# Cross attention with state and a routed MoE on one core: six x tiles, four transposed ones that lend their first to the state, and a redrawn order of work

## The chip, the cores and the metric

The kernel runs on one core of one Trainium2 chip. A core has five engines that run side by side and meet through semaphores: TensorE (PE in the profile; its weight loads are listed apart as PEld), VectorE (DVE), ScalarE (ACT), GpSimd (POOL) and SyncE (SP), which here only issues DMAs. Each engine executes its own instructions in the order in which the program has them, so an instruction that waits holds up everything behind it on its engine. The metric is the device time of one execution in microseconds (us). The kernel before takes 752.19 us as the median of three runs (751.41 to 753.65).

## The reference

Two stages follow each other. In the first, every one of 8 batches and 8 heads has 512 tokens `x` and 32 state rows, 64 wide; the tokens read from the state and the state reads from the tokens. In the second, the 4352 rows that result, 512 wide, pass through 8 experts, weighted by a Sinkhorn-normalised gate over all rows.

```python
scores = scale * x @ state^T;   a  = softmax(scores);   xread = a  @ state
scores2 = scale * state @ x^T;  a2 = softmax(scores2);  sread = a2 @ x
x = concat([xread, sread]) as (B*(512+32), H*64)         # 4352 x 512
P = exp(logits - logits.max());  logits = x @ w_gate     # over all rows
for _ in range(8):
    P /= P.sum(1) + 1e-9;  P /= P.sum(0) + 1e-9;  P *= N / E
out = sum over e of  P[:, e] * (relu(x @ w1[e]) @ w2[e])
```

The result does not need `xread` itself: `xread @ w1` is `a @ (state @ w1)`. The kernel multiplies state and w1 once per expert and batch (V) and uses the transposed softmax `aT` as the other factor; the gate goes the same way with G, which is state times the gate's weights.

## The kernel before, in words

**Two halves.** The first half, some 135 us, is the attention of all batches together with the whole of expert 0 and the beginning of expert 1. Its order on every engine is written out by hand in a table, `PLAN`: each entry is the number of an operation and a letter for its engine (P TensorE, V VectorE, A ScalarE, G GpSimd, S the SP queue, H bookkeeping without an instruction). `issue` (L105) walks through the table. The operations are built by calls of `op` with the engines that may take them and a price for each; the prices serve whoever draws the table, and no instruction depends on them. The second half, experts 1 to 7, is an ordinary loop at the end of the program: for each expert and block of rows, `layer2` forms seven half-size products instead of eight (A, E and Bseed in the profile), while `layer1` and `project` feed the next block.

**Attention.** For a batch `b`, two loads on the GpSimd queue (L468) bring x as fp16 into a tile `x_nat`. There are four such tiles. x is transposed to `xT` (three tiles): by TensorE for the first two batches (L578, with copies out of PSUM), by DMA transposes on the SP queue for the others (L591). A batch is worked on in two parts of four heads. For each part TensorE forms scores (psB, L605). VectorE then transposes them in blocks (L628), takes the maximum (L631), subtracts it (`subA`, L648); ScalarE takes the exponential (L656), VectorE the sum and its reciprocal, and VectorE or GpSimd multiplies (`a`, L670). VectorE turns the result into `aT` (L674). On the other side VectorE takes a maximum over the scores in PSUM (L640), ScalarE the exponential E with its sum (L652), VectorE the reciprocal (L659), and VectorE or GpSimd scales E (`normB`, L662). A DMA transpose on the SP queue turns E into ETs (L742), and TensorE reads the state's new rows with it (su, L758), which `keepS` (L764) copies into `xsT`. The two parts of the first batch take a direct way: TensorE forms the scores a second time in the other layout (psA, L684) and transposes `a` itself (L709).

**State and weights.** The state is loaded into `st_st`, cast into `st_in` (both tiles of their own in a pool `spl`, L435), and transposed by TensorE into `stT` (L492). Expert 0's weights come in four loads on the GpSimd queue (`weights_ops`, L535): w1 in two, w2 in two.

**Expert 0.** V is formed by TensorE (v_ps, L870) and copied out by ScalarE or VectorE; hidden products (hps, L897) are copied out through a relu into `hT` (L425, L427); the second layer (yps, L935) is copied into `acc`.

**Gate and Sinkhorn.** After all `aT` and su, the last of the gate products (L788, the one on `xsT`) gives the last logits. Then VectorE takes the global maximum (lmx, L814) and runs eight rounds: `rownorm` (five instructions on VectorE as one operation), a product with ones on TensorE (csb, L846), `colnorm` (three instructions as one operation). `sums_w` (L959) forms on VectorE the eight sums of expert 1's second weight that the seven products need.

**PSUM.** In the first half six banks are shared in turn by all products other than psB: a product takes the bank whose last reader was issued longest ago. In the second half there are fixed banks A, E, B0 and B1 and four for hidden products. `seed` (L351) opens B0 and B1 with a product of the identity; ScalarE then copies A over B0 (L363).

**The end.** `layer2_last` (L299) finishes the state's rows: two groups of 128 rows, the second in two halves of the columns, with VectorE adding into `acc` (L314) and eight DMAs of 64 KB on the SP and ScalarE queues, four for each group of rows (L317).

Of the kernel before, what the change touches and what calls it, by code (L numbers as in the profile page):

```python
# [17 lines left out]
46V 62P 50H 51G 61A 71V 63P 60A 52G 64V 11G 72V 73A 80P 65V 12G 435P 401P 66A 81V 13H 79P 14G 82V 436A 88V  # L18
437A 404P 83A 67V 402A 137H 403A 89V 96H 97P 100P 84V 406A 68V 90A 98A 15G 85V 69P 86P 53G 405A 99V 87V 70A
103P 101A 102A 91V 409P 16H 92G 413P 104V 407P 410A 411P 105V 111A 438P 120P 414V 408A 419P 421P 106V 415P  # L20
112V 138S 121V 74V 439A 412A 422V 113V 417P 107A 54G 440A 75G 122V 432P 429P 123V 370V 420A 469P 128A 418A
416A 17G 108V 140P 124A 125V 423P 426P 471A 433P 114A 148V 93S 129V 430P 149V 172H 424P 76S 434A 115V 470A
109G 130V 139S 110V 126G 141V 131A 427P 18G 127V 142V 428V 431A 445P 143V 132V 94P 150A 95V 77P 425A 156P 116G
447P 151V 133V 78V 449P 446A 443P 441P 144A 455P 164V 152G 448A 117S 19H 450V 157V 444A 165V 173S 442A 451P
456A 166A 134S 20G 452A 453P 463P 158V 472P 207H 145V 175P 159V 183V 184V 457P 31G 146G 454A 176V 473A 160A
464P 185A 174S 460P 458P 461P 465A 147V 161V 21G 153S 177V 191P 47P 162G 474A 118P 167V 459A 154P 462A 178V
163V 135P 49A 168G 199V 22H 48V 179A 466P 136A 352P 475P 200V 192V 201A 193V 119V 467P 476A 194V 23G 195A 485P
202V 208S 210P 180V 169S 155A 218V 356P 353A 481P 357V 468A 487P 219V 24G 489P 181G 186V 211V 242H 486A 482A
477P 490V 488A 483P 479P 220A 170P 478A 503P 187G 480A 484V 171A 203G 196V 537P 209S 25H 212V 226P 197G 504A
505A 506P 213V 500P 182V 198V 26G 234V 221V 507A 222V 204S 188S 491P 27G 538A 227V 539A 501P 497P 502A 508A  # L30
492P 235V 243S 228V 244S 214A 229V 511P 215V 236A 523P 230A 498P 494P 216G 245P 495P 515P 512V 499A 277H 231V
524A 493A 517P 246V 253V 223S 496A 247V 521P 516A 237V 254V 519P 509P 522V 518A 248V 513P 232G 189P 520A 255A
205P 510V 224P 514V 540P 28H 278S 261P 249A 190V 269V 29G 225A 270V 262V 531P 534P 206V 238G 250V 532P 256V
358P 271A 535P 217V 541A 533A 233V 542A 312H 279S 263V 272V 536A 354P 280P 528P 543P 529P 525P 288V 289V 251G
555P 264V 281V 265A 282V 239S 257V 526P 359A 266V 544A 530V 556A 545P 355A 547P 549P 273G 553P 527A 546V 571P
313S 290A 548A 283V 605P 550A 554V 296P 267G 606V 304V 572A 305V 240P 573A 557P 284A 607A 558A 551P 297V 552A
568P 360P 258S 241V 285V 30G 291V 306A 559P 562P 574P 298V 252V 315P 299V 286V 569P 576A 268V 323V 563P 575A
274S 300A 560P 570A 292G 316V 361A 561A 581P 564A 307V 565P 362P 324V 317V 301V 325A 302G 566P 363V 582A 326V
579P 587P 583P 287V 314S 588V 591P 567A 580A 639P 608P 584A 592A 347H 303V 331P 577P 348G 641V 640A 610A 609A
339V 293S 589P 585P 275P 332V 259P 578A 327G 586A 260A 590A 294P 340V 308G 333V 341A 593P 309S 318V 319A 334V  # L40
295V 364P 594P 276V 328S 625P 619P 342V 595A 335A 365A 599P 320V 602P 343V 336V 600P 337V 603P 626A 321G 322V
329P 310P 350G 344S 601A 349G 311A 620V 345P 338V 346V 604V 366P 596P 330A 368P 369V 351G 597P 367A 371V 611P
372P 598A 695H 615P 617P 373V 612V 374P 375V 613P 614V 616A 623P 618A 621P 696H 711H 376A 705P 377V 642P 624A
622A 706A 707A 630P 643V 697V 708P 644A 378P 379V 631P 710A 627P 698V 380V 647P 632A 709A 636P 628P 381P 633P
699V 648V 637P 382V 634P 657P 629A 638A 383V 700V 653P 658A 655P 384P 651P 635A 701V 654A 725P 385V 723P 386V
702V 656A 726A 716P 652A 724A 717A 645P 659P 649P 714P 646A 650A 660A 387P 721P 715A 712P 727P 687P 722A 388V
728A 688A 667P 713A 664P 389V 390P 703V 665P 668P 391V 673P 674A 392V 661P 670P 669A 729V 393P 671P 394V 666A
662P 672A 677P 395V 718P 663A 678A 679P 675P 683P 719A 681P 720V 680A 676A 685P 396P 684A 682A 397V 686A 692P
704V 689P 693P 690P 730P 398V 694A 399P 733P 731V 691A 732A 735A 734A 400V
# [68 lines left out]
def kernel(  # L118
# [63 lines left out]
    outs = out.rearrange("(b s) d -> b s d", s=SB)[:, S:, :]  # L182
# [32 lines left out]
    axp = actx.enter_context(tc.tile_pool(name="attn_x", bufs=4))  # L215
    axt = actx.enter_context(tc.tile_pool(name="attn_xt", bufs=3))
# [46 lines left out]
    def layer1(e, bi):  # L263
# [35 lines left out]
    def layer2_last():  # L299
# [4 lines left out]
        nb = 128 // Ns  # L304
        for row in range(tn // 128):
# [10 lines left out]
            for i in range(nb):  # L316
                (nc.scalar if i % 2 else nc.sync).dma_start(  # L317
                    out=outs[row * nb + i], in_=acc[ds(i * Ns, Ns), k, :])

    def layer2(e, bi, n):  # L320
# [30 lines left out]
        def seed(i):  # L351
            bb = bank([128, 2, DH], FP32, "Bseed", "B%d" % i)
            nc.tensor.matmul(bb.rearrange("p c d -> p (c d)"), identh, aT[:, 0, 0], start=True, stop=True)
            seeds.append(bb)

        if not n:
            for k, eng in enumerate(("DVE", "ACT", "DVE", "POOL")):
                weigh(k, eng)
        product(A, h(0, 0), w2h[:, :NJ, :DH], True)
        if not n:  # L360
            seed(0)
        Bb = seeds[n % 2]
        nc.scalar.copy(out=Bb[:, :nk], in_=A[:, :nk])  # L363
        yield
        product(Eb, s(0), T[:, 0], True)
        if not n:
            seed(1)
# [67 lines left out]
    st_in = spl.tile([128, B, NQ, 2, D], FP16, name="st_in")  # L435
    st_st = spl.tile([128, B, NQ, D], FP32, name="st_st")
    loads = []
    for g in range(2):
        def load(g=g):
            bs = ds(g * B // 2, B // 2)  # L440
            (nc.scalar if g else nc.sync).dma_start(
                out=st_st[:, bs], in_=state[bs].rearrange("b (q h) n d -> (h n) b q d", q=NQ))

        loads.append(dma((0, 0), 1.0, load, lands=2.7))
        ops[-1].since, ops[-1].hard = 0.5, 1
# [14 lines left out]
    xn = [slot(axp, 4, [128, H, NSC * D], FP16, "x_nat") for _ in range(B)]  # L460
# [18 lines left out]
    for g in range(2):  # L479
        for s_ in range(2):  # L480
# [4 lines left out]
            bd.append(op((0, 0, g), {"DVE": (0.50, 0.64)} if s_ else {"ACT": (0.50, 0.65)}, place, loads[g:g + 1] + warmed))  # L485
    stT_ready = []
    for g in range(4):
# [10 lines left out]
        t = op((0, 1, g), {"PE": (0.35, 0.55)}, turn, bd[g // 2 * 2:g // 2 * 2 + 2] + [makeh], [ps])  # L498
# [68 lines left out]
    for b in range(B):  # L567
        xT = slot(axt, 3, [128, H * NSC // 2, 128], FP16, "xT")
# [29 lines left out]
        for q in range(NQ):  # L598
# [62 lines left out]
            def normB(eng, E2=E2, rrec=rrec):  # L661
                engines[eng].tensor_scalar(out=E2.tile, in0=E2.tile, scalar1=rrec.tile, scalar2=None,  # L662
                                           op0=ALU.mult)
# [59 lines left out]
            n2 = op(r(3), {"DVE": (0.10, 0.25)}, biasB, [m2], [nsB], [nmB])  # L723
# [5 lines left out]
            f2 = op(r(6), {"DVE": (0.16, 0.26)}, recB, [e2], [rrec], [rowsum])  # L729
            f2 = op(r(6), {"DVE": (0.35, 0.48), "POOL": (1.56, 1.70)} if POOLB else {"DVE": (0.35, 0.48)}, normB, [f2], [], [E2, rrec])  # L730
# [33 lines left out]
            def keepS(eng, b=b, q=q, su=su):  # L764
                copy(eng, xsT[:, ds(2 * q, 2), ds(b * Ns, Ns)], su.tile)
# [38 lines left out]
    def sk(on, emit, after, **how):  # L804
        return op(rank, on, lambda _: emit(), after, **how)
# [6 lines left out]
    op((30.0,), {"DVE": (0.2, 0.3)}, lambda _: nc.vector.memset(ones128, 1.0))  # L812
# [8 lines left out]
    c = sk({"PE": (0.18, 0.45)}, lambda: nc.tensor.matmul(gb.tile, ones128[0:1, :], sm_["gm"]), [c], takes=[gb])  # L821
# [4 lines left out]
    for it in range(8):  # L826
        def rownorm():
            rsum = tile_of("rsum", [128, NTB])
            nc.vector.reduce_sum(out=rsum, in_=Pmat, axis=AX_X)
            nc.vector.tensor_scalar(out=rsum, in0=rsum, scalar1=EPS, scalar2=None, op0=ALU.add)  # L830
# [279 lines left out]
```

## Time and profile before

| what | value |
|---|---|
| median of three runs | 752.19 us (751.41 to 753.65) |
| the profiled execution: its time | 752.75 us |
| the profiled execution: its span | 751.0 us |
| TensorE busy | 736.0 us (98%) |
| VectorE busy | 617.0 us (82%) |
| ScalarE busy | 517.7 us (69%) |
| GpSimd busy | 70.8 us (9%) |
| first transpose of x on TensorE | 6.86 us |
| first hidden product of expert 0 (L897) | 18.86 us |
| last gate product (on xsT) begins | 99.47 us |
| first product on A of expert 1 | 135.14 us |
| last addition into acc begins | 747.02 us |

The span is the time between the first and the last instruction of the profiled execution; the time around it is 1.75 us. A row of the list of groups names the line, the engine, the operation, and output and inputs by the program's names with their shapes and the number of instructions; then come their busy time, the mean of one in ns, and the idle time of the engine just ahead of them with what ended it. In the timeline the two first columns are the start and the length in us of neighbouring instructions that were merged. PEclk is the share of its full speed at which TensorE's clock was granted; where no record has been made yet it is shown as full.

### The profile page before, as it was taken

How to read it: one execution, taken by the hardware profiler on the slowest of the kernel's cores; microseconds unless marked ns; L12 is line 12 of the kernel's file. 1: busy time of each engine (PE TensorE's matmuls, PEld its weight loads, DVE VectorE, ACT ScalarE, POOL GpSimd, SP SyncE). 2: the span in 40 equal slices, each digit the busy share in tenths (PEclk: the TensorE clock that was granted, in tenths of full speed). 3: DMA queues.
4: the chain of work that ended last, by engine and by line, in shares of the span. 5: the costliest groups of instructions: out<-in, count | busy, mean ns of one | idle time of the engine just before them, and what ended most of it. 6: DMA issues, size and time to landing. Idle time of an engine off the chain costs nothing.

```text
span 751.0 us, 16151 instructions
## 1 busy us (share of the span) xinstructions
PE 736.0 (98%) x6517; PEld 502.2 (67%) x6517; DVE 617.0 (82%) x1529; ACT 517.7 (69%) x1014; POOL 70.8 (9%) x81
## 2 busy tenths in 40 slices
PE   5999999999999999999999999999999999999997
PEld 3444445666777777776776767776777767767776
DVE  5899989877888789788888788887897888887885
ACT  6876856799876766667666766667666676667662
POOL 4674410200010000100000000100001000000000
PEclk9899999999999999999999999999999999999999
DMA  9997560600033000700007000330007000002234
GB/s 179 140 134 131 82 99 1 109 6 1 1 61 53 2 1 2 113 1 2 1 2 112 2 1 1 58 57 1 1 2 112 2 1 2 1 31 94 103 113 141
DMA packets 51323, 36.71 MB, mean 49 GB/s; under 512 B 25392, under 2 KB 43824, under 8 KB 51248
## 3 DMA queue, kind: packets, MB, share of 16 engines
q0 software_dynamic: 22272, 20.97, 18.5%
q1 hardware_dynamic: 27744, 14.18, 7.6%
q8 instruction: 51, 0.84, 0.5%
q10 hardware_dynamic: 1232, 0.52, 0.3%
q14 instruction: 24, 0.20, 0.1%
HBM read 42.48 MB, written 8.91 MB: 68 GB/s over the span
## 4 chain that ended last, share of the span: by engine, by line
PE 92%; DVE 3%; DMA 1%; ACT 1%; POOL 1%; issue 0%; SPq 0%; POOLq 0%; DVEq 0%; ACTq 0%
PE hps L255 28%; PE Bseed L334 20%; PE A L334 14%; PE E L334 14%; PE yps L935 6%; PE hps L897 4%; PE v_ps L235 4%; DMA xT<-x_nat 1%; DMA x_nat<-in_x_dram 1%; PE y L312 0%; PE v_ps L870 0%; POOL a L670 0%; ACT Hm L275 0%; DVE acc L348 0%; POOL E L662 0%; PE su_ps L758 0%
## 5 line engine op out<-in xcount | busy, mean ns | idle before, releaser
L275 ACT ACTIVATE Hm<-hps 128x512 f16<-128x512 f32 (+1 forms) x496 | 265.8, 577 | 130.5 <-PE hps L255 128.1
L255 PE MATMUL hps<-aT,V 128*128 128x512 f16 x880 | 230.6, 379 | 0.0
L334 PEld LDWEIGHTS <-Hm 128*128 128x128 f16 x1888 | 181.6, 98 | 71.3 <-issue 15.9
L348 DVE SCALAR_TENSOR_TENSOR acc<-Bseed,Pmat,acc 128x256 f32<-128x256 f32 x354 | 155.0, 477 | 9.8 <-PE Bseed L334 6.9
L334 PEld LDWEIGHTS <-sm 128*128 128x128 f16 x1416 | 138.3, 98 | 34.5 <-issue 0.3
L334 PE MATMUL A<-w2h,Hm 128*128 128x256 f16 x944 | 123.7, 273 | 0.0
L334 PE MATMUL Bseed<-T,Hm 128*128 128x256 f16 x944 | 123.3, 273 | 0.0
L255 PEld LDWEIGHTS <-V 128*128 128x128 f16 x880 | 86.1, 98 | 50.8
L348 DVE SCALAR_TENSOR_TENSOR acc<-E,Pmat,acc 128x256 f32<-128x256 f32 x236 | 103.2, 476 | 13.8 <-PE E L334 13.5
L281 DVE TENSOR_TENSOR sm<-Hm 128x512 f16<-128x512 f16 (+1 forms) x122 | 50.1, 411 | 60.4 <-ACT Hm L275 60.2
L243 ACT CAST V<-v_ps 128x512 f16<-128x512 f32 x144 | 74.2, 612 | 0.0
L348 DVE SCALAR_TENSOR_TENSOR acc<-A,Pmat,acc 128x256 f32<-128x256 f32 x118 | 51.9, 479 | 17.9 <-PE A L334 17.6
L935 PE MATMUL yps<-w2h,hT 128*128 128x512 f16 x272 | 64.1, 379 | 0.1
L334 PE MATMUL E<-w2h,sm 128*128 128x256 f16 x472 | 61.7, 273 | 0.0
L334 PE MATMUL E<-T,sm 128*128 128x256 f16 x472 | 61.6, 273 | 0.0
L334 PE MATMUL Bseed<-T,sm 128*128 128x256 f16 x472 | 61.5, 272 | 0.0
L363 ACT COPY Bseed<-A 128x512 f32<-128x512 f32 (+1 forms) x62 | 34.1, 550 | 37.9 <-PE A L334 35.3
L282 DVE TENSOR_TENSOR Hm<-Hm 128x512 f16<-128x512 f16 (+1 forms) x122 | 50.3, 412 | 4.2
L284 DVE TENSOR_TENSOR sm<-Hm,sm 128x512 f16<-128x512 f16 (+1 forms) x122 | 50.2, 412 | 4.2
L283 DVE TENSOR_TENSOR sm<-sm,Hm 128x512 f16<-128x512 f16 (+1 forms) x122 | 49.4, 405 | 0.0
L194 POOL DMA_DIRECT2D w1h<-in_moe_w_dram x12 | 8.5, 714 | 396.9 <-PE hps L255 396.5
L935 PEld LDWEIGHTS <-hT 128*128 128x128 f16 x272 | 25.4, 99 | 28.9 <-issue 1.8
(127 smaller groups left out, 617.7 us busy)
## 6 DMA issues: line engine op xcount, KB each, us to landing
w1h<-in_moe_w_dram POOLq DMA_DIRECT2D x16, 512.0 KB, 7.0
w2h<-in_moe_w_dram POOLq DMA_DIRECT2D x16, 512.0 KB, 8.4
out_dram<-acc SPq DMA_DIRECT2D x32, 256.0 KB, 2.5
x_nat<-in_x_dram POOLq DMA_DIRECT2D x16, 256.0 KB, 5.6
st_st<-in_state_dram ACTq DMA_DIRECT2D x1, 256.0 KB, 4.9
st_st<-in_state_dram SPq DMA_DIRECT2D x1, 256.0 KB, 4.2
ETs<-E SPq DMA_TRANSPOSE x16, 4.3
out_dram<-acc SPq DMA_DIRECT2D x4, 64.0 KB, 1.8
```

Source lines behind the costliest of these rows:

```text
L235: nc.tensor.matmul(ps[q][ds(j * Ns, Ns), :], stT[ds(r, 64), bi, q, ds((j ^ q) * Ns, Ns)], w1h[ds(r, 64), 2 * q + j // 2, cols], tile_posit ...
L243: nc.scalar.copy(out=dst, in_=src)
L255: nc.tensor.matmul(out, lhs, rhs, start=(k == 0), stop=(k == len(terms) - 1))
L275: nc.scalar.activation(out=Hm[:, i, j, :tn], in_=hps[:, :tn], func=AF.Relu)
L281: nc.vector.tensor_add(s1, a21, a22)
L282: nc.vector.tensor_sub(a21, a11, a21)
L283: nc.vector.tensor_sub(s2, s1, a11)
L284: nc.vector.tensor_sub(s4, a12, s2)
L334: nc.tensor.matmul(dst[:, c], lhs(j, c), rhs[:, j], start=first and c == 0 and j == 0, stop=(j == NJ - 1), skip_group_check=True)
L348: nc.vector.scalar_tensor_tensor(out=dst, in0=src[:, c], scalar=p[:, k], in1=dst, op0=ALU.mult, op1=ALU.add)
L363: nc.scalar.copy(out=Bb[:, :nk], in_=A[:, :nk])
L935: nc.tensor.matmul(yps.tile, hT[fb].tile[:, ds(tk * 128, 128)], w2h[:, fb, :], start=(fb == 0), stop=(fb == NFB - 1))
```

## The change

The changed kernel differs in these points:

- `attn_x` has six tiles and `attn_xt` four. `st_st` takes the first turn in the ring of x tiles, `st_in` the first in the ring of xT tiles; the pool `spl` holds neither any more.
- The table is another one. In it expert 0's two loads of w2 stand behind each other on the GpSimd queue, with nothing but the making of the 32-bit identity between them; before, an E product of GpSimd stood between them.
- `issue` puts products of the identity with itself ahead of five operations (`IDLE`): 50 ahead of the first turning of x, 3 ahead of each of the two psA products, 14 ahead of a v_ps product and 5 ahead of the first aT transposes. They are transposes where the PSUM tile is fp16 (the 50 and the 5) and plain products where it is fp32 (the 3, 3 and 14). Their results are overwritten.
- GpSimd may do `subA`, and the table gives it all 14 of them; `normB` on GpSimd is a product of two tensors with the reciprocal broadcast, no longer a product with a scalar per row; six of the eight T sums go to GpSimd.
- Sinkhorn's rounds are single operations, one for each instruction, so that the table can put other work between them.
- `seed` is gone. The first hidden product of the second half is formed in B0 (`lent`), and the copy of A to B0 follows its relu.
- The state's rows are kept in `xsT` in another order, so that a group of 128 rows leaves in one DMA: one for the first group, two, one for each half of the columns, for the second.

```diff
-def issue(ops):
+def issue(ops, idle):
     for step in PLAN:
...
+        idle(op.takes[0].tile if op.takes else None, IDLE.get(int(step[:-1]), 0))
         op.emit(ENGINES[step[-1]])
...
+IDLE = {56: 50, 63: 3, 80: 3, 452: 14, 69: 5}
...
-    axp = actx.enter_context(tc.tile_pool(name="attn_x", bufs=4))
-    axt = actx.enter_context(tc.tile_pool(name="attn_xt", bufs=3))
+    axp = actx.enter_context(tc.tile_pool(name="attn_x", bufs=6))
+    axt = actx.enter_context(tc.tile_pool(name="attn_xt", bufs=4))
...
-    def layer1(e, bi):
+    def layer1(e, bi, lent=None):
...
-                hps = bank([128, S], FP32, "hps", "h")
+                if lent is None:
+                    hps = bank([128, S], FP32, "hps", "h")
+                else:
+                    hps, lent = lent, None
...
-            for i in range(nb):
-                (nc.scalar if i % 2 else nc.sync).dma_start(
-                    out=outs[row * nb + i], in_=acc[ds(i * Ns, Ns), k, :])
+                (nc.scalar if c + 1 < parts else nc.sync).dma_start(
+                    out=outs[row, :, :, cols], in_=acc[:, k, cols])
...
-        def seed(i):
-            bb = bank([128, 2, DH], FP32, "Bseed", "B%d" % i)
-            nc.tensor.matmul(bb.rearrange("p c d -> p (c d)"), identh, aT[:, 0, 0], start=True, stop=True)
-            seeds.append(bb)
...
-    st_in = spl.tile([128, B, NQ, 2, D], FP16, name="st_in")
-    st_st = spl.tile([128, B, NQ, D], FP32, name="st_st")
+    early = [Slot(rings.setdefault("xT", Ring(4)),
+                  lambda: axt.tile([128, B, NQ, 2, D], FP16, name="st_in", tag="xT")),
+             Slot(rings.setdefault("x_nat", Ring(6)),
+                  lambda: axp.tile([128, B, NQ, D], FP32, name="st_st", tag="x_nat"))]
...
             def normB(eng, E2=E2, rrec=rrec):
-                engines[eng].tensor_scalar(out=E2.tile, in0=E2.tile, scalar1=rrec.tile, scalar2=None,
-                                           op0=ALU.mult)
+                if eng == "POOL":
+                    nc.gpsimd.tensor_mul(E2.tile, E2.tile, rrec.tile.broadcast_to((128, S)))
+                else:
+                    nc.vector.tensor_scalar(out=E2.tile, in0=E2.tile, scalar1=rrec.tile, scalar2=None, op0=ALU.mult)
...
-                s1 = op(r(4), {"DVE": (0.60, 0.80)}, subA, [m1], [], [eA, mxA])
+                s1 = op(r(4), {"DVE": (0.60, 0.80), "POOL": (1.05, 1.20)}, subA, [m1], [], [eA, mxA])
...
-        c = sk({"DVE": (2.10, 2.25)}, rownorm, [c])
+        for emit, us, tail in ((row_sums, 0.43, 0.03), (row_eps, 0.20, 0.03), (row_rec, 0.37, 0.03),
+                               (row_mul, 0.45, 0.03), (col_part, 0.62, 0.15)):
+            c = sk({"DVE": (us, us + tail)}, emit, [c])
...
-        nc.vector.tensor_sub(T[:, i, jj], p[:, jj], q[:, jj])
+        engines[eng].tensor_sub(T[:, i, jj], p[:, jj], q[:, jj])
...
+    def idle(t, n):
+        if not n:
+            return
+        t = t.rearrange({2: "p a -> p a", 3: "p a b -> p (a b)", 4: "p a b c -> p (a b c)"}[len(t.shape)])[:, :128]
+        for _ in range(n):
+            if t.dtype == FP16:
+                nc.tensor.transpose(t, identh, identh)
+            else:
+                nc.tensor.matmul(t, identh, identh, start=True, stop=True, skip_group_check=True)
```

More of the change, by code (lines that the diff above doesn't have):

```diff
@@ L459 @@
     makeh.since, makeh.hard = 0.7, 1
-    xn = [slot(axp, 4, [128, H, NSC * D], FP16, "x_nat") for _ in range(B)]
+    xn = [slot(axp, 6, [128, H, NSC * D], FP16, "x_nat") for _ in range(B)]
     x_ready = []
@@ L811 @@
     part("ones")
[L812 removed]
+    ones = op((30.0,), {"DVE": (0.1, 0.25)}, lambda _: nc.vector.memset(ones128, 1.0))
     part("K")
@@ L970 @@
     tdone = op((due_1, 1), {"HOST": (0.0, 0.0)}, make_t, [room] + w2_ready(1))
[L971 to L974 removed]
+    for g in range(2):
+        tg = []
+        for i in range(4):
+            tg.append(op((due_1, 1), {"DVE": (0.42, 0.52), "POOL": (1.06, 1.20)}, lambda eng, i=i, g=g: sums_w(eng, i, g),
+                         [tdone] + tg[i - 1:i] * (i == 1) + tg[1:2] * (i == 3)))
+            tg[-1].goal = -0.9
     for bi in range(2):
@@ L1055 @@
             next(v, None)
+        if not i:
+            seeds += [bank([128, 2, DH], FP32, "Bseed", "B%d" % k) for k in range(2)]
         l2 = layer2(e, bi, i)
-        l1 = layer1(*work[i + 1]) if i + 1 < len(work) and work[i + 1] not in hid else iter(())
+        l1 = iter(())
+        if i + 1 < len(work) and work[i + 1] not in hid:
+            l1 = layer1(*work[i + 1], None if i else seeds[0].rearrange("p c d -> p (c d)"))
+        if not i:
+            next(l2)
+            next(l1)
         for k in range(7):
```

152 lines of the change are left out of this document (80 added, 72 removed).

## The prediction

> **What bounds the kernel now.** I read the page's table by engine first, then its slices, then the busy time by stretches of 10 us, the same for TensorE by single microseconds, the list of waits, the timelines of the first 60 us and of the end, and last the groups by line.
>
> ```profile
> PE 736.0 (98%) x6517; PEld 502.2 (67%) x6517; DVE 617.0 (82%) x1529; ACT 517.7 (69%) x1014; POOL 70.8 (9%) x81
> ...
> PEclk9899999999999999999999999999999999999999
> ```
> TensorE (PE) is busy in all but 15 us. Those 15 us, and the slices where the granted clock is under full, are what an edit ahead of the second expert can win; from 135 us on both programs issue nearly the same TensorE work.
>
> ```profile
> 10.00:20.00 10.00, 7.86 (x96) 4.29 (x94) 9.05 (x22) 8.50 (x19) 0.83 (x1) 0.80 1.35 201
> 20.00:30.00 10.00, 10.00 (x68) 3.73 (x67) 8.29 (x21) 7.53 (x16) 6.10 (x7) 0.86 1.10 154
> 30.00:40.00 10.00, 10.00 (x97) 4.65 (x96) 9.67 (x23) 9.15 (x20) 7.03 (x8) 1.00 0.91 112
> 50.00:60.00 10.00, 8.99 (x83) 3.83 (x80) 9.77 (x20) 7.37 (x17) 5.40 (x6) 1.00 1.03 134
> ```
> (Stretch, length, busy PE, PEld, DVE, ACT, POOL, clock, DMA share, GB/s.) Behind 20 us VectorE (DVE) is nearly as full as TensorE: 93% busy from 30 to 100 us. Two engines share the bound of the attention stage, and relief for one alone buys little.
>
> ```profile
> 15.00:16.00 1.00, 0.25 (x5) 0.97 1.45 195
> 16.00:17.00 1.00, 1.00 (x8) 0.50 1.44 194
> 22.00:23.00 1.00, 1.00 (x19) 0.62 1.16 210
> 14.63 0.62 PE L578 MATMUL xT_ps<-identh,x_nat 128*128 128x128 f16 x8
> 16.00 1.03 PE L578 MATMUL xT_ps<-identh,x_nat 128*128 128x128 f16 x8 [0.76 <-DMA x_nat<-in_x_dram]
> 18.86 3.57 PE L897 MATMUL hps<-aT,V 128*128 128x512 f16 x8
> ```
> After thin work at 13 to 16 us the clock falls to 0.50 at about 15.95 and is back at 22.76. Eight transposes cost 0.62 us warm, 1.03 cold; the first hidden products take 3.5 us up to the next group (22.36), where eight of them at 86.59 take 1.73.
>
> ```profile
> PE xT_ps L578 <- DMA x_nat<-in_x_dram: 7.6, 2, 6.9
> PE psB L605 <- DMA xT<-x_nat: 1.3, 2, 0.9
> PE v_ps L870 <- ACT V L419: 0.5, 1, 0.5
> 41.96 1.17 DVE L648 TENSOR_TENSOR eA<-eA,mxA 128x512 f32<-128x512 f32 x1
> L648 DVE TENSOR_TENSOR eA<-eA,mxA 128x512 f32<-128x512 f32 x14 | 10.4, 746 | 0.1
> L662 POOL TENSOR_SCALAR E<-E,rrec 128x512 f16<-128x512 f16 x12 | 19.2, 1600 | 19.5 <-DVE rrec L659 15.3 <-ACT hT L425 4.0
> L670 POOL TENSOR_TENSOR a<-eA,rA 128x512 f16<-128x512 f32 x12 | 12.8, 1066 | 21.6 <-DVE rA L667 12.9 <-DVE logits L421 4.2 <-ACT logits L419 2.4
> 746.06 2.30 SPq L317 DMA_DIRECT2D out_dram<-acc  x4
> 747.02 0.48 DVE L314 SCALAR_TENSOR_TENSOR acc<-y,Pmat,acc 128x256 f32<-128x256 f32 x1 [0.39 <-PE y L312]
> ```
> TensorE's waits after 6.86 us, when the first x lands, sum to under 5 us.
>
> **The change part by part.** The profiled execution took 752.75 us (span 751.0 and 1.75 around it), 0.56 above the median of 752.19. The sum is made against 752.75.
>
> *Fillers and the first 23 us.* 50 transposes of the identity are put ahead of the first turning of x. The identity is made by 1.29 us; at the cold 107 ns each (16 state transposes from 7.68 to 9.39) they end by 6.7, before x lands at 6.86: no cost. Later 6+14 plain products and 5 transposes go into gaps. If the clock then holds, the eight hidden products cost 1.73 instead of 3.50 and the eight v_ps beside them 0.23 instead of 0.40: 1.9 won. In the new order the 64 small G products (0.72 us at 42.5 us) and 16 more v_ps (about 0.6) run before the first hidden product: 1.3 of later work done in slack. But ScalarE now has eight V evictions before the copy of aT that hidden products wait for, not six (2 x 0.53 more), and one xT copy less (0.63), and the second turning of block 1 waits for an eviction to free its bank: they start 0.4 to 0.9 later than 18.86, I take 0.7. The six fillers at psA hold the first max up by about 0.2. Sum -1.9 -1.3 +0.7 +0.2 = **-2.3**. Ends: -0.8 if the spell stays (three cold microseconds, half lost), -3.3 if the clock is up from the first x on.
>
> The evidence on what wakes the clock is thin. TensorE is transposing for most of 16.00 to 18.45 and the clock stays at 0.50 until 22.76, after hidden products have run for a while; the warm stretch before it followed psB, psA and v_ps products. That speaks for plain products. The Trainium skill (TensorE: Matmul & The Clock Gate, Part 4: PE-mode transpose) says that transposes do not count as activity for the gate; the trace leans that way. By that rule the 50 would wake nothing, and the term would lie between -0.8 and -2.3.
>
> *Work moved between engines ahead of the last gate product (99.47 us).* Counted from both orders, up to the global max of the logits: VectorE loses 14 subtractions (10.4 us), two hidden evictions (1.4) and an xsT copy (0.2); it gains four `a` products (4 x 0.67), two E products (2 x 0.33) and three xT copies (3 x 0.42). That is 7.4 us by mean rows. The rows overlap at their ends (they sum to 95.3 for 85.1 busy), so 6.7. ScalarE loses four acc copies, two hidden evictions, one V copy and three xT copies, near 6. TensorE issues 28 fewer yps, 6 fewer hps and 16 fewer v_ps there: 28 x 0.216 + 6 x 0.216 + 0.6 = 7.9 us, which now stands behind the gate. So the gate must come 7.9 us earlier only to break even. VectorE was 85.1 us busy up to 100, 83.5 of it in the 91.8 us behind 8.35 (91%); at that density the 76.8 us left end near 92. TensorE's work behind its first hidden product, counted at warm spacing (0.216 for 512 columns), filled 96.6% of the time to the gate with the cold loss taken out; at that density the gate comes at 88. That is 7.4 or 11 us earlier. With both nearly full I take the middle: against TensorE's pace **+1.2** of idle. Ends: 0 and, with VectorE alone as the pace, +3.5; with a starving chain more (below).
>
> POOL gets those 14 subtractions at about 1.05 us (L670) and 10 E products whose form changes: 1.60 each before; a tensor product of the same size took 1.07, so between 1.05 and 1.6, and I take 1.07. With 20 DMA issues of 0.8 us that is near 50 us of POOL's first 90. Behind a subtraction that waits for VectorE's max, on the one POOL queue, stand the x loads and the E products that the SP queue's transposes wait for.
>
> *Six x tiles and four xT tiles.* Loads and DMA transposes may run one block further ahead. In before, SP issues the second transpose of block 2 at 26.83 us behind two ETs transposes; now it stands behind one. The waits of psB for xT (1.3) and for E (0.3) may go: **-1.0**, ends 0 and -1.6. The second half of w2 is issued at about 8 us, not 20.70; no listed wait names it, so 0; should it crowd out x of block 1, the cover is gone and TensorE's wait at 16.00 (0.76) grows by at most its own transfer, 3 us.
>
> *Sinkhorn in single steps; T sums on POOL (6 of 8).* Behind the gate TensorE now has 41 us of work, VectorE 36 by rows and ScalarE 26, where it was 33, 34 and 25 in 35.7 us. The eight rounds (30 us) get room: **-0.5**, ends 0 and -1.3 (the excess of that stretch).
>
> *Handing over.* Two seed products go (0.22 each), one hidden group is drawn forward into a seed bank, and the copy into that bank now waits for its relu (0.6): **-0.3**, ends +0.3 and -0.5. *End.* Behind the last acc product one DMA is issued on SP instead of two in turn (0.58 each), but of 128 KB instead of 64 (landings 2.5 at 256 KB, 1.8 at 64): **-0.3**, ends +0.2 and -0.6.
>
> Sum: -2.3 +1.2 -1.0 -0.5 -0.3 -0.3 = -3.2: 752.75 - 3.2 = **749.5 us**, 2.7 under the median.
>
> **The rivals.**
> - *POOL starves VectorE (slower).* A subtraction is 0.4 us longer on POOL and may stand behind a 0.8 us issue or a 1.07 us product. For it: POOL in order, half full. Against: two pairs are in flight. If VectorE stands still 0.4 us for each of 14 pairs, the idle term is 5.6 instead of 1.2: 753.9; with a collision of 0.49 us (the subtraction at 41.96 took 1.17 while POOL ran L670) for four of the eight `a` products left on VectorE, 755.9. I name it **755**. It decides when the last gate product comes less than about 5 us earlier than 99.47. The Trainium skill (SBUF — State Buffer, on the shared port pair) states the collision as a lock: a VectorE operation with two SBUF inputs and a POOL operation that reads SBUF exclude each other. Two of the 14 subtractions, at 1.17 us, agree.
> - *VectorE sets the pace, as dense as before.* Idle +3.5 instead of +1.2: **751.8**. For it: 93% busy; against: 6.7 us less of it.
> - *The fillers do not hold the clock.* The spell stays and the first term is -0.8: **751.0**. For it: 2.5 us of mostly transposes at 16 us left the clock at 0.50, and 55 of the 75 fillers are transposes; against: 14 plain products fall just where the thin work was.
> - *All named waits go.* -3.3, 0, -1.6, -1.3, -0.5, -0.6: -7.3, **745.5**. Against: TensorE was nearly full behind 23 us, and POOL's chain is longer.
>
> **How the numbers follow.** My forecast 0.40 (own range 747.3 to 751), VectorE's pace 0.16, POOL 0.18, the cold clock 0.12, all waits gone 0.14. Two runs differ by up to 2.2 us, so a measurement tells about 0.3% (2.3 us) from no change: under 749.9 is faster, over 754.4 slower. Faster: the 0.14 and most of the forecast, 0.52; slower: POOL's 0.18; within: 0.30. The range 745.7 to 754.8 leaves out 2 in 10.
>
> **What would show it.** Right: no 0.50 rows between 16 and 23 us; last gate product near 90 us; first product on A near 132 to 133; VectorE's subtraction group gone and POOL near 60 us busier work before 100; one DMA behind the last acc product. Wrong: `eA` waits on POOL in VectorE's or ScalarE's list, a gate product after 94 us, clock 0.50 after 16 us, or psB still waiting for xT.

## The result and the profile after

The changed kernel takes 754.27 us (median of 22 runs, 751.98 to 759.49); the kernel before, run beside it on the same chip, takes 752.62 (22 runs, 751.41 to 754.26). The ratio is 1.0031, with a 95% interval of 1.0020 to 1.0042: slower by 0.3%. The forecast was 749.5 us, faster than before.

The profiled execution of the changed kernel took 751.98 us (span 750.2), which is the fastest of its 22 runs and by no means a typical one. Three more profiles of the same kernel, from the runs below, have spans of 753.6, 752.4 and 753.0. All four are used in what follows.

First the page of the changed kernel, its table by engine and the row of the granted clock:

```profile
PE 737.9 (98%) x6590; PEld 506.0 (67%) x6590; DVE 612.6 (82%) x1523; ACT 514.8 (69%) x1006; POOL 78.8 (11%) x95
...
PEclk9999999999999999999999999999999999999999
```

VectorE lost 4.4 us in all and GpSimd gained 8. No slice of the clock is under nine tenths any more. In the stretches of 10 us (columns as in the prediction) the change of place is seen:

```profile
10.00:20.00 10.00, 6.97 (x171) 4.46 (x171) 9.38 (x23) 8.84 (x20) 1.74 (x2) 1.00 1.35 201
20.00:30.00 10.00, 7.20 (x60) 2.98 (x58) 6.68 (x17) 5.88 (x13) 6.72 (x8) 0.96 1.43 146
30.00:40.00 10.00, 10.00 (x99) 4.43 (x98) 8.21 (x21) 7.53 (x18) 5.62 (x6) 0.87 1.43 170
```

The clock is full from 10 to 20 us, where it was 0.80. But from 20 to 30 us TensorE is busy for 7.20 us only, where it had been busy throughout, and behind that the clock falls. The DMA engines' share is 1.43 in the two stretches from 20 to 40, where it was 1.10 and 0.91 (it adds up the times of all packets over 16 engines, so it can pass 1). TensorE's timeline names the place:

```profile
28.25 0.30 PE L612 MATMUL psB<-xT,stT 64*32 64x256 f16 x8 [2.80 <-DMA xT<-x_nat]
```

And its list of waits behind 7 us (us in total, times, longest):

```profile
PE psB L612 <- DMA xT<-x_nat: 3.4, 2, 2.8
PE v_ps L893 <- DMA w1h<-in_moe_w_dram: 1.9, 2, 1.6
PE xT_ps L585 <- DMA x_nat<-in_x_dram: 0.7, 1, 0.7
```

TensorE comes to the first scores of block 2 at 25.45 us, and waits 2.8 us for the DMA transpose of that block's x. The kernel before came there at 26.77 and did not wait; its row names no wait:

```profile
26.77 0.29 PE L605 MATMUL psB<-xT,stT 64*32 64x256 f16 x8
```

The four profiles agree on this place (psB at 28.25, 28.41, 28.5 and 28.3) and differ behind it: the last gate product comes at 91.79, 95.22, 94.02 and 94.58 us. From there to the first product on A it is 42.89 us in each of them. So what spreads the times of this kernel lies ahead of the gate.

Two of the groups that moved, up to 100 us:

```profile
L655 POOL TENSOR_TENSOR eA<-eA,mxA 128x512 f32<-128x512 f32 x14 | 14.6, 1046 | 20.7 <-DVE mxA L638 16.6 <-DVE nsB L651 3.7 <-DVE rrec L666 0.2
L670 POOL TENSOR_TENSOR E<-E,rrec 128x512 f16<-128x512 f16 x10 | 10.4, 1043 | 10.9 <-DVE rrec L666 10.1 <-issue 0.5
```

And from the end of the timeline, the last DMAs of the SP queue:

```profile
745.34 2.05 SPq L323 DMA_DIRECT2D out_dram<-acc  x2
```

The subtractions on GpSimd take 1046 ns and the E products, now a product of two tensors, 1043 instead of 1600, both as forecast. GpSimd waits for VectorE, and not the other way round. At the end two DMAs are issued on SP where there were four, and one on ScalarE's queue where there were four.

### The profile page after: what moved, and what is told of

It reads as the page before. It is cut to its first block, busy times and chain, and to the rows that moved or that the text cites. A ratio compares the mean times of both kernels' runs of the same rounds, so it can differ in the third digit from the quotient of the medians.

```text
span 750.2 us, 16283 instructions
## 1 busy us (share of the span) xinstructions
PE 737.9 (98%) x6590; PEld 506.0 (67%) x6590; DVE 612.6 (82%) x1523; ACT 514.8 (69%) x1006; POOL 78.8 (11%) x95
## 3 DMA queue, kind: packets, MB, share of 16 engines
q0 software_dynamic: 22272, 20.97, 19.1%
## 4 chain that ended last, share of the span: by engine, by line
PE 92%; DMA 4%; DVE 1%; POOL 1%; ACT 1%; issue 0%; POOLq 0%
PE hps L260 28%; PE Bseed L340 20%; PE A L340 14%; PE E L340 14%; PE yps L958 7%; PE hps L920 4%; PE v_ps L240 4%; DMA x_nat<-in_x_dram 3%; DMA xT<-x_nat 1%; PE su_ps L767 1%; PE y L319 0%; PE v_ps L893 0%; DVE acc L354 0%; ACT Hm L283 0%; POOL x_nat L475 0%; PE gate_ps L797 0%
## 5 line engine op out<-in xcount | busy, mean ns | idle before, releaser
L354 DVE SCALAR_TENSOR_TENSOR acc<-E,Pmat,acc 128x256 f32<-128x256 f32 x236 | 103.2, 477 | 14.5 <-PE E L340 14.3
L958 PE MATMUL yps<-w2h,hT 128*128 128x512 f16 x272 | 65.9, 386 | 0.1
```

The costliest lines, as they stand in the source:

```text
L354: nc.vector.scalar_tensor_tensor(out=dst, in0=src[:, c], scalar=p[:, k], in1=dst, op0=ALU.mult, op1=ALU.add)
L958: nc.tensor.matmul(yps.tile, hT[fb].tile[:, ds(tk * 128, 128)], w2h[:, fb, :], start=(fb == 0), stop=(fb == NFB - 1))
```

## The experiments

The runs fall into four groups; those of a group ran on one chip beside the kernel before (752.97, 752.66, 752.69 and 752.70 us in the four). Times are medians, ratios are against the kernel before of the same group.

| run | edit | us | ratio (95%) | last gate product in its profile |
|---|---|---|---|---|
| e1 | changed kernel | 753.25 | 1.0012 (0.9996 to 1.0029) | 95.22 |
| e2 | w2's second half late | 752.80 | 1.0008 (0.9990 to 1.0025) | 96.85 |
| e3 | subtractions on VectorE | 761.32 | 1.0108 (1.0092 to 1.0124) | 100.86 |
| e4 | no fillers | 754.72 | 1.0029 (1.0010 to 1.0049) | 95.26 |
| e5 | x loads spaced | 752.51 | 0.9999 (0.9989 to 1.0008) | 91.37 |
| e6 | xT ahead of ETs | 753.67 | 1.0032 (1.0015 to 1.0048) | 97.02 |
| e7 | kernel before, w2 early | 752.88 | 1.0005 (0.9995 to 1.0015) | 99.02 |
| e8 | e5 and e6 together | 750.52 | 0.9975 (0.9964 to 0.9985) | 91.29 |
| e9 | changed kernel | 755.82 | 1.0036 (1.0024 to 1.0048) | 94.02 |
| e10 | fillers in the wait | 755.16 | 1.0027 (1.0010 to 1.0043) | 97.08 |
| e11 | kernel before, five x tiles | 752.49 | 0.9997 (0.9989 to 1.0006) | 98.45 |
| e12 | e8 with w2 late | 753.25 | 1.0008 (0.9998 to 1.0018) | 94.90 |
| e13 | changed kernel | 756.27 | 1.0052 (1.0034 to 1.0069) | 94.58 |
| e14 | e8 again | 750.28 | 0.9968 (0.9956 to 0.9980) | 89.99 |
| e15 | e8 without fillers | 754.48 | 1.0027 (1.0014 to 1.0039) | 93.80 |
| e16 | e8 with block 3's loads early | 754.77 | 1.0032 (1.0017 to 1.0047) | 94.45 |

**First group: which part of the change loses.** e1 is the changed kernel itself. The others change the table or the fillers:

```diff
 e2: w2's second half (54G) behind GpSimd's first E product (75G)
-... 488A 54G 487V 48V 75G 17G 104V ...
+... 488A 487V 48V 75G 54G 17G 104V ...
 e3: the 14 subtractions back to VectorE
-106G 123G 143G 159G 178G 194G 213G 229G 248G 264G 283G 299G 318G 334G
+106V 123V 143V 159V 178V 194V 213V 229V 248V 264V 283V 299V 318V 334V
 e4:
-IDLE = {56: 50, 63: 3, 80: 3, 452: 14, 69: 5}
+IDLE = {}
```

> The changed kernel as it is, for a second profile, since its 22 runs lie between 751.98 and 759.49 us and the profile at hand is of the shortest. Theory D (DMA): the DMA transposes of block 2 wait until the weight and x loads have drained, TensorE stands 2.8 us or more at psB near 25 us, and the stall lets the clock fall: a longer run shows a longer stall at psB or a second cold spell, with the last gate product (91.8 us in the first profile) later by as much. Theory P (POOL): the subtractions on POOL starve VectorE: a longer run shows VectorE idle between 30 and 90 us instead, with no longer DMA wait.

> The changed kernel with one move: the load of the second half of expert 0's second weight stands behind the first E product of POOL again, as before (issue near 19 us instead of 8.8). Theory D: 0.5 MB at about 200 GB/s is 2.6 us that the transposes of block 2 no longer wait for; the wait of psB for xT near 25 us (2.8 us) goes to under 0.5, the cold spell at 29 us (3.4 us, half lost) goes with it, and the time falls by 2 to 4 us against the changed kernel, to 750 to 752. Theory P: no change beyond 1 us, since POOL keeps its subtractions.

> The changed kernel with the 14 subtractions of the attention back on VectorE (0.68 us each), all else and the order unchanged. Theory P: VectorE stops waiting for POOL and the time falls by 2 us or more. Theory D: the wait of psB for xT near 25 us stays (over 2 us); VectorE, which has 9.5 us more to do ahead of the last gate product, makes that product later by 3 to 6 us, and the time rises by 1 to 5 us, as far as TensorE ran out of work for it.

> The changed kernel without the 75 fillers on TensorE. If the fillers carry the early gain, the clock is at half from 6.3 us up to some 10 to 12 us or to 22 us, the first hidden product comes 1 us or more later than 18.3 us, and the time rises by 1 to 3 us. If the stall at psB near 25 us eats that gain anyway (theory D: the transposes land when the loads have drained, whatever TensorE did before), the time stays within 1 us.

e3 is 8 us slower than e1. The subtractions on GpSimd do not starve VectorE: in the changed kernel VectorE's list of waits names GpSimd nowhere, and only ScalarE waited for a subtraction, 1.2 us in all. A caution: with the subtractions gone, GpSimd issues the loads of x block 3 at 19.1 and 19.9 us instead of 19.2 and 22.3, and the profile of e3 has the longest wait for xT of all (4.7 us, ahead of the first scores of block 3; from its list of waits):

```profile
PE psB L613 <- DMA xT<-x_nat: 6.1, 2, 4.7
```

So the 8 us, more than was expected, are not VectorE's part alone, and e3 does not tell that part from the one of the loads. In e2 the first wait vanished (psB of block 2 at 25.25 us), but later ones took its place: yps waited 1.9 us for w2, the second part of block 2 waited 1.7 us for its transpose and the first part of block 3 waited 3.4, and the gate came no earlier. That profile is of the longest of e2's 12 runs, though (757.01; the shortest took 750.93). The intervals of e1 and e2 overlap widely, so the gain of 2 to 4 us that was expected did not come, and a smaller one is not ruled out. e4 against e1 puts the 75 fillers at 1.5 us, with intervals that overlap, less than the 2.3 that the forecast had given their part: yps began at 24.16 us without them and at 22.92 (e1) with them, so the early gain is real, and it was gone by the gate (95.26 against 95.22 in these two profiles).

**Second group: the transfers.** What arrives late is the DMA transpose of x, so the loads that share the DMA engines with it were moved. In e5 the x loads of blocks 3 to 7 stand later in GpSimd's order; here are GpSimd's entries alone (the bookkeeping entry of block 7's xT tile moves behind its load, too). In e6 the second transpose of block 2 (139S) goes ahead of the first transpose of E (76S) on the SP queue. e7 moves one load in the kernel before.

```diff
 e5
-54G 75G 17G 106G 18G 123G 109G 116G 126G 20G 143G 21G 23G 159G 146G 168G 178G 29G 187G 24G 194G 133G
+54G 75G 106G 17G 123G 109G 116G 126G 18G 143G 20G 159G 21G 146G 168G 23G 178G 187G 24G 194G 133G 29G
 e6
-138S ... 76S 139S
+138S 139S ... 76S
 e7 (kernel before)
-53G 92G 54G 75G
+53G 54G 92G 75G
```

> The changed kernel with the loads of x blocks 3 to 7 set later in POOL's order, to about the times that they had in the kernel before (two near 23 and 28 us, then one every 4 to 5 us); six x tiles stay, they are only not filled at once. Theory D (bulk loads that are issued early stand ahead of the DMA transposes of x, and TensorE then waits for xT): the DMA share from 30 to 60 us falls from 1.43/1.30/1.24 to near 1.1, psB's waits for xT behind 30 us go, the last gate product comes at or before 91.5 us in most runs, and the time is 1 to 2.5 us under the changed kernel's (751 to 752). The wait of psB at 25 us, which belongs to w2, stays. Rival V (TensorE's pace is set by VectorE and the softmax chain; the DMA waits only show who is late): nothing changes, 753 to 754.

> The changed kernel with one step moved on the SP queue: the second DMA transpose of x block 2 ahead of the first transpose of E instead of behind it. Theory D: it is issued at 19.3 instead of 21.8 us, but its packets still stand behind the second half of w2 until about 22, so psB at 25.45 waits less, by the 1.2 to 2.4 us of the ETs transpose that no longer stands between, and the last gate product comes 0 to 2 us earlier: 752 to 753.5. If xT's lateness were only the order on SP, the wait would go altogether and the cold spell behind it too: 750 to 751.5. Rival V: no change, 753 to 754.

> The kernel before with one step moved: expert 0's second half of w2 is loaded right behind the first half (about 8 us instead of 20.70). Nothing else of the change. Theory D: the DMA transpose of x block 2 that is issued at 17.3 us gets its packets only at about 22 instead of 20, psB of block 2 (26.77 us in the kernel before) starts 0.5 to 2.5 us later or waits for xT, and the time is 0.5 to 2.5 us longer than before. Rival (the load is hidden in any order): no change, within 0.5 us of before, since the first yps are not bound by w2.

> Both: the x loads spaced as in e5 and the second transpose of block 2 ahead of ETs as in e6. Theory D: the two gains add, the last gate product comes near 89 to 90 us, and the time is 749.5 to 751.5, under the kernel before by 1 to 3 us. Rival V: 753 to 754, as the changed kernel.

With the loads spaced (e5) the loss is gone: 752.51, level with the kernel before. It came about the other way round than expected: the wait for block 2, which was to stay as w2's, shrank from 2.8 to 0.4 us, and a wait behind 30 us, which was to go, was there (2.2 us, for block 3 at 35.57). Both edits together (e8) give 750.52, under the kernel before with the whole interval. The early transpose by itself (e6) gains nothing while the loads are early, and 2.0 us once they are spaced (e8 against e5). In the profile of e6, which is of the longest of its nine runs, psB waits 2.4 us for xT and 4.1 us for E, where E in its turn had waited for a transpose of ETs that now stands behind. e7 missed its expectation in the time and met it in the transfer: the first transpose of block 2 takes longer, and nobody waits for it. From the lists of DMA issues between 17 and 19 us (the last figure is the time to landing), first the kernel before:

```profile
xT<-x_nat SPq DMA_TRANSPOSE x1, 5.7
```

The same row of e7:

```profile
xT<-x_nat SPq DMA_TRANSPOSE x1, 8.3
```

Issued at 17.3 and 17.1, it landed at 23.0 and 25.4 us. TensorE wanted it at 26.8 and 26.5.

**Third group: the kernel before with early loads, the cold clock, w2 once more.** e9 is the changed kernel. e10 puts 36 plain filler products ahead of the psB products that wait. e11 gives the kernel before a fifth x tile and issues the loads of blocks 3 and 4 earlier (there is no room for six there, since the state keeps tiles of its own); of its table GpSimd's entries are shown. e12 is e8 with w2's second half behind GpSimd's first E product.

```diff
 e10
-IDLE = {56: 50, 63: 3, 80: 3, 452: 14, 69: 5}
+IDLE = {56: 50, 63: 3, 80: 3, 452: 14, 69: 5, 140: 36}
 e11 (kernel before)
-    axp = actx.enter_context(tc.tile_pool(name="attn_x", bufs=4))
+    axp = actx.enter_context(tc.tile_pool(name="attn_x", bufs=5))
-54G 75G 17G 109G 126G 18G 116G 152G 20G 31G 146G 21G
+54G 17G 18G 75G 109G 20G 126G 21G 116G 152G 31G 146G
 e12 (e8)
-54G 75G 106G 17G
+75G 54G 106G 17G
```

> The changed kernel once more, as the base for the runs beside it. 753 to 754.5. In the traces so far the time from the last gate product to the first product on A is 42.9 us in every one, so whatever differs lies ahead of the gate.

> The changed kernel with 36 more filler products (plain, 128 columns, about 2 us) on TensorE right ahead of the first psB products of x block 2, which is where TensorE waits 2 to 3 us for xT at about 25.5 us. Nothing becomes earlier by it. Theory D with a second step (a wait of 2 us and more is followed by a spell of 3.4 or 6.8 us at half clock, which costs half of it): the spell behind that wait goes, and the time is 1 to 2 us under the changed kernel's. Rival (the spells cost nothing, as TensorE waits for others then anyway, or they come from other waits): no change, or 0.5 us longer.

> The kernel before with five x tiles instead of four and the loads of blocks 3 and 4 issued earlier (block 3 at about 21 us, right behind w2, instead of 25.5 and 29.7; block 4 from about 28 instead of 35.6 and 39.1). Nothing else of the change; xT keeps three tiles. Theory D: the first transpose of block 2, issued at 17.3, still lands at about 23, but the second (issued near 27) and those of block 3 stand among the x loads and land 1 to 3 us later than 31.2 and 37.6; TensorE waits for xT and the time is 0.5 to 2 us longer than before. Rival (loads run ahead for nothing, but harm nothing): within 0.5 us of before.

> The kernel of e8 (x loads spaced, second transpose of block 2 ahead of ETs) with w2's second half issued behind POOL's first E product as well, at about 19 us. Theory D: the first transposes of block 2 land 2 us earlier (near 24.5 instead of 26.7), psB of block 2 no longer waits, but w2 lands near 27 and the first yps wait for it: up to 2 us there (1.9 in e2). 750 to 751.5, no clear gain over e8. If w2's early load was the chief cause: 749 or less.

e10 was a miss. In its profile the clock stays full over the first wait, as meant, and until 40.86 us; then other waits bring a spell of 6.8 us. Its interval and that of e9 overlap, and nothing is decided on what a spell costs. e11 was a miss as well: early loads alone do the kernel before no harm. They land at 27.9, 29.5, 32.1 and 34.9 us, and the first transpose of block 2 takes 5.7 us as before, presumably because w2's second half is still issued at 20.3, when that transpose has got its first packets (20.24), and the loads of x stand behind w2. e12 missed its 750 to 751.5 and shows why w2 belongs early in the new order: the transpose landed at 23.1 us, and then yps waited for w2 (from its list of waits):

```profile
PE yps L959 <- DMA w2h<-in_moe_w_dram: 3.6, 1, 3.6
```

**Fourth group: side by side on one chip.** e13 is the changed kernel and e14 the kernel of e8. e15 takes the fillers out of e8, and e16 puts block 3's two loads (17G, 18G) back to where the changed kernel has them.

```diff
 e15 (e8)
-IDLE = {56: 50, 63: 3, 80: 3, 452: 14, 69: 5}
+IDLE = {}
 e16 (e8)
-75G 106G 17G 123G 109G 116G 126G 18G
+75G 17G 106G 18G 123G 109G 116G 126G
```

> The changed kernel, unedited, beside the runs of the same call. 753 to 755.5, 0.1 to 0.4% over the kernel before.

> The kernel of e8 (x loads spaced, second transpose of block 2 ahead of ETs) once more. Theory D: 750 to 751.5, 2 to 4 us under the changed kernel of the same call and 1 to 3 under the kernel before. Had e8 only been lucky: between the two, 752 to 753.

> The kernel of e8 without the 75 filler products. Theory D says that the changed kernel could not use its early start, because xT of block 2 came late anyway (there the fillers were worth 1.5 us at most, e4 against e1). With xT earlier the early start should be worth more: 1.5 to 2.5 us, so 752 to 753.5. If the fillers do nothing beyond the first 23 us: 750 to 751.

> The kernel of e8 with the two loads of x block 3 back at their early places (about 19 and 22 us), the loads of blocks 4 to 7 still spaced. If it is block 3's loads that delay the transposes of block 2: these land near 28 and 33 again instead of 26.7 and 27.9, TensorE waits at 25 to 28 us, and 752 to 754. If it is the loads of blocks 4 and 5 (28 to 33 us) among the transposes of block 3: as e8, 750 to 751.5.

e14 is 6.0 us faster than the changed kernel (750.28 against 756.27), by the order of the loads and of one transpose alone. The changed kernel's medians in the groups lie between 753.25 and 756.27; by the ratios of its 22 runs and of e8 the difference is 4.2 us. e16 loses 4.5 of these again, by two loads. Stretches of e13:

```profile
20.00:30.00 10.00, 7.18 (x58) 2.85 (x57) 6.54 (x16) 5.95 (x13) 7.10 (x8) 0.88 1.42 150
30.00:40.00 10.00, 8.01 (x62) 3.34 (x60) 7.69 (x20) 7.11 (x16) 4.89 (x6) 0.94 1.61 138
24.00:26.00 2.00, 1.52 (x14) 0.45 (x13) 1.39 (x6) 1.95 (x5) 1.42 (x2) 1.00 1.55 92
```

The same of e14:

```profile
20.00:30.00 10.00, 9.20 (x69) 3.86 (x68) 8.88 (x21) 6.05 (x13) 7.69 (x9) 1.00 1.28 169
30.00:40.00 10.00, 7.44 (x91) 3.75 (x91) 7.71 (x22) 8.73 (x21) 6.55 (x9) 1.00 1.30 173
24.00:26.00 2.00, 1.41 (x21) 0.45 (x19) 1.29 (x4) 1.94 (x4) 1.25 (x3) 1.00 1.28 162
```

From 24 to 26 us e13's DMA engines are busier (1.55 against 1.28) and move 92 GB/s instead of 162. With the stretch from 40 to 50 us (9.89 and 10.00) TensorE is 25.1 us busy in e13 and 26.6 in e14, from 20 to 50 us, 1.6 less; and e13 has two spells of 3.4 us at half clock (from 27.7 and 41.3 us), where e14's clock is full from 4.74 us to the end. TensorE stands still for the first 0.6 us of the first spell, so half of 6.2 us is lost in them, 3.1. That is 4.7 us, against 4.6 between the two gate products. How much of that is a spell's own price, which a held clock would win back by itself, stays open after e10.

TensorE's timeline in e14 around the place of the wait:

```profile
25.93 0.30 PE L613 MATMUL psB<-xT,stT 64*32 64x256 f16 x8 [0.59 <-DMA xT<-x_nat]
```

And the first lines of e14's list of waits:

```profile
PE su_ps L768 <- DMA ETs<-E: 1.6, 1, 1.6
PE v_ps L894 <- DMA w1h<-in_moe_w_dram: 1.5, 2, 1.3
PE psB L613 <- ACT E L660: 1.3, 2, 0.8
PE psB L613 <- DMA xT<-x_nat: 1.0, 2, 0.6
```

In e14 no wait is longer than 1.6 us, and psB begins when its transpose lands. e15 answers what became of the fillers' gain: in e8 they are worth 4.2 us (754.48 against 750.28, more than the 1.5 to 2.5 expected), in the changed kernel 1.5 at most, which its noise does not tell from nothing. Of the 4.2 us, 1.6 stand at the first yps (22.25 in e14, 23.87 in e15); where the rest comes from was not tried. The fillers do not always hold the clock: in the profiles of e6 and e8, which have them all, it is at half from 14.5 to 17.9 us and from 14.9 to 18.3.

e14's kernel is faster than both that were to be compared: by 6.0 us than the changed one, and by 0.32% (0.20 to 0.44) than the one before.

## Why the prediction was wrong

**The step that failed** is "Six x tiles and four xT tiles", forecast at -1.0 with ends 0 and -1.6, and with it the second half of w2 at 0. I reckoned that loads which may run ahead let waits for xT go. They made them longer: psB waits 3.4 to 5.3 us for xT in the profiles of the unedited changed kernel, where it was 1.3. The landing times of block 2's first transpose, read from the lists of DMA issues, show how it came about:

| kernel | w2's second half issued | block 3's loads issued | transpose issued | landed | psB begins |
|---|---|---|---|---|---|
| before | 20.7 | 25.5, 29.7 | 17.3 | 23.0 | 26.8 |
| e7: before, w2 early | 8.2 | 25.3, 29.5 | 17.1 | 25.4 | 26.5 |
| e11: before, loads early | 20.3 | 21.1, 21.9 | 17.4 | 23.1 | 25.3 |
| e14: spaced | 8.8 | 22.2, 28.0 | 17.8 | 25.9 | 25.9 |
| e16: block 3 early | 8.8 | 19.4, 22.2 | 17.8 | 28.5 | 28.5 |
| changed | 8.8 | 19.2, 22.3 | 17.9 | 28.2 | 28.2 |

In the kernel before, the transpose landed 3.8 us ahead of its use. The change spent this slack three times: TensorE came 1.3 us earlier, w2's second half in front of the transpose cost 2.4 (e7), and block 3's loads beside it 2.6 (e16 against e14). These sum to 6.3, which is 2.5 over the slack, and the wait was 2.8. Each is smaller than the slack; e7 shows one of them hidden. e11 is no such test of the loads: there they did not delay the transpose at all (23.1). I had looked for a wait on w2 or on x of block 1 and found none; the victim was a third transfer, which waited in nobody's list because it was 3.8 us early.

The landing row of the changed kernel, again from the issues between 17 and 19 us:

```profile
xT<-x_nat SPq DMA_TRANSPOSE x1, 10.3
```

That of e14:

```profile
xT<-x_nat SPq DMA_TRANSPOSE x1, 8.1
```

And that of e16, which is e14 with block 3's loads early:

```profile
xT<-x_nat SPq DMA_TRANSPOSE x1, 10.6
```

The forecast named "psB still waiting for xT" as a sign of its being wrong, but no rival had it as its mechanism. The chance of 0.18 for slower belonged to GpSimd starving VectorE, which VectorE's list of waits refutes.

**Fillers and the first 23 us** (-2.3): no stretch from 16 to 23 us is at half clock in this profile, as forecast, but the gain was larger than the term. yps begins at 22.35 instead of 24.72, 2.4 earlier, and by then TensorE has also done 64 G, 8 gate and 8 v_ps products that stood behind it before, about 1 us. That is some 3.4, the end of -3.3 that was given for a clock that is up from the first x on, as it was here. The hidden products did not begin 0.7 later than 18.86 but 0.5 earlier (18.34); without fillers they begin at 20.16 (e4) and 19.86 (e15). What was wrong was to carry the gain on to the end without asking what stood ready at the place where TensorE would arrive. In the order of e8, where psB waits 0.2 to 1.0 us in all for xT, the fillers bring 4.2 us.

**Work moved ahead of the last gate product** (+1.2 of idle, gate near 90): in e14 the last gate product comes at 89.99, 9.5 us earlier than before, and the first product on A at 132.88, inside the 132 to 133 that was named. In the changed kernel they come at 91.8 to 95.2 and at 134.7 to 138.1. The size of the moved work holds; the waits for xT stood in its way.

**Sinkhorn in single steps** (-0.5): from the gate to A it is 42.89 us where it was 35.67, and 7.9 us of TensorE work had been moved there: 0.7 less than the sum. **Handing over** (-0.3): from A to the first y 607.95 instead of 608.21, -0.26. **The end** (-0.3): from the first y to the end of the span 7.57 instead of 7.62, nearly nothing. The last DMA is issued 4.22 us behind the first y instead of 4.59, but it is of twice the size, and the span ends 3.35 us behind that issue instead of 3.03.

With the loads spaced and one transpose moved, the changed kernel takes 750.28 and 750.52 us in two groups, and the forecast was 749.5. Against the kernel before of their groups that is 2.4 and 2.1 us less, where the sum said 3.2. So the sum was near what these parts are worth, and the change as made did not let them be had. The agreement at the gate is in part luck: up to the first yps TensorE won about 1 us more than forecast, and behind it e14 lost somewhat more than that, with 3.9 us of waits of psB and su for ETs, E and xT in its list. Whether the rest is **VectorE's pace** (751.8 as a rival) was not tried: VectorE is 65 to 77% busy from 20 to 50 us in e13, where it waits for the same transfers, and in e14 77 to 89% there and 93 to 98% from 50 to 90.

## What to carry to other kernels

A transfer that appears in no list of waits is not free to move things past: read when it lands and when it is first used, and count the difference as a slack that every edit draws on, the ones that make its reader earlier among them. More buffers let loads be issued earlier, and that is a loss where they share the DMA engines with a transfer that is needed first; the issue order of loads and transposes, not the number of tiles, was worth 4 to 6 us here. Where a part of a change has done its work locally and the total does not move, test it again in a version without the next wait: the fillers were worth 1.5 us at most in one order and 4.2 in another.

## What the runs showed of the hardware

**Transposes alone bring the clock up.** The forecast weighed a rule of the Trainium skill (TensorE: Matmul & The Clock Gate, Part 4: PE-mode transpose), that transposes do not count as activity for the gate. This case shows the opposite, and the measurement decides. In the changed kernel TensorE runs nothing but the 50 transposes of the identity from 0 to 6 us; the granted clock goes to full at 5.35 us, its first record (the column of the clock shows 1.00 ahead of it, too). By single microseconds:

```profile
4.00:5.00 1.00, 1.00 (x12) 1.00 (x11) 0.43 (x1) 0.50 (x1) 1.00 (x2) 1.00 1.45 184
5.00:6.00 1.00, 1.00 (x18) 1.00 (x15) 0.43 (x1) 0.74 (x2) 1.00 (x2) 1.00 1.43 185
```

And from the timeline the first eight transposes of x behind them, at their warm time:

```profile
6.29 0.62 PE L585 MATMUL xT_ps<-identh,x_nat 128*128 128x128 f16 x8
```

Twelve to thirteen transposes a microsecond up to 5 us become 18 from 5 to 6. In the other profiles with fillers full clock comes between 4.1 and 7.2 us, and at 12.1 to 12.5 in the two variants of the changed kernel without them. In the kernel before and its variants it came at 9.8 to 12.5.

**DMA transposes stand behind a full stream of loads, and mix badly with it.** The transpose issued at 17.92 us in the changed kernel moves its first packet at 21.84, when the stream of loads, at about 200 KB a microsecond until then, has just begun to thin; in the kernel before, issued at 17.27, it moves the first at 20.07, when that stream ends. The Trainium skill (DMA: Bandwidth & Descriptors, Queues, rings and completion order) has the DMA engines take turns, packet by packet, between the queues that they have work for; while the loads ran at full rate the traces show no turn for the transposes. Whether the transposes' packets stood ready by then no trace here shows. Later both do interleave, and then both are slow: from 24 to 26 us the 92 GB/s at a share of 1.55 in e13 against 162 at 1.28 in e14, in the rows above, and 109 at 1.61 in e16.

**E products on GpSimd** take 1043 ns as a product of two tensors and 1600 as a product with one scalar per row, at the same size.
